# A retention-and-feed-forward kernel: pieces as two halves of 64 tokens, with all their matmuls in four 64x64 tiles

## The chip, the cores and the metric

The kernel runs on one core of a Trainium2 chip. The metric is device time in microseconds: the median of several runs of the whole program, inputs and outputs in HBM. A profiled execution of the kernel before gives the trace; "the profile" is its page, and the views named below (the chain that ended last, groups of instructions, waits, timeline) are answers of that trace.

## The reference

Inputs `q`, `k`, `v` have 8 sequences (batch), 8 heads, 576 tokens and 64 dimensions a head, in fp32. The kernel computes a retention (attention without softmax, decaying with distance) and feeds it to a dense block with a hard-swish:

```python
scores = scale * np.matmul(q, k.transpose(0, 1, 3, 2))          # scale = 1/8
gamma = 1.0 - 2.0 ** (-5.0 - np.arange(H))                      # one decay for each head
rel = pos[:, None] - pos[None, :]
Dmat = np.where(rel >= 0, gamma[:, None, None] ** rel[None, :, :], 0.0)
attn = np.matmul(scores * Dmat, v)                              # B, H, S, D
x = attn.transpose(0, 2, 1, 3).reshape(B * S, H * D)            # 4608 x 512
h = x @ w_in                                                    # 512 x 2048
out = (h * np.clip(h + 3.0, 0.0, 6.0) / 6.0) @ w_out            # 2048 x 512
```

## The kernel before

**Dense part.** The 4608 tokens are nine blocks of 512 (blocks 0 to 7 are the first 512 tokens of each sequence, block 8 holds the last 64 tokens of all eight). For each block `gemm1` runs 16 units `g1` (four 512-column matmuls, L401, into a PSUM bank `ph`; ScalarE's `u` L408 and VectorE's `gt` L409 form the activation), and 16 units `g2` follow (four 512-column matmuls, L459, into `pout`; after four units ScalarE copies `pout` to `osb`, L463, and SP stores it). The operands are fp16.

**Attention part.** The tokens are 36 pieces of 128: four main pieces for each sequence, and four rest pieces (12, 21, 30, 35) that hold the last 64 tokens of two sequences each. Because the decay is a power of the distance, a piece needs its own scores under a causal mask and a running state (keys times scaled values, a 64x64 matrix for each head) of the pieces before it. Four pairs of heads share the 128 partitions. For a piece the kernel does:

- `scores`: 8 matmuls of 128 columns, 64 rows by 128 columns of the array (L302, and L583 for the second piece of a pair), then the mask on VectorE (`at`, L306 or L591);
- `inter`: state times queries, with the state laid out block-diagonally in `tbd` so that both heads of a pair go through one 128x128 matmul (L324);
- `intra`: 8 matmuls of 128 columns, 128 rows by 64 columns of the array (L335), accumulated onto `inter`, then one ScalarE copy to `xt16` (L341);
- `update_mm`: 8 matmuls of 64 columns, 128 rows by 64 columns (L359), and `update_state`: an add and a scaling on VectorE (L375, L376), and two ScalarE copies of the state into `tbd` (L388, L389).

**Order.** It is written out by hand; the engines run their queues in order, and TensorE's order is the order of the code. Pieces 0 to 3 (`EARLY`) run first, while loads arrive: their Q and K are transposed on TensorE (`k_by_pe` L215, `q_by_pe` L224), piece 3 has forms of its own (`scores_last`, `out_last`), and the state is summed in PSUM by an identity matmul (`state_early`, L273 and L277) and multiplied by `gfull` (L282). `warm` matmuls (L174) fill gaps. Then comes `gemm1(0)`. Pieces 4 to 7 are worked between the `g2` units of block 0 by `first_step`, and the first units of block 1 are split into a group of 384 and one of 128 columns (`g1_columns`, L424), the first of which needs only pieces 4 to 6. Pieces 8 to 35 are worked in pairs by `step(ended, begun)` between the `g2` units of the block before theirs, at the positions in `AT`; a pair never spans two blocks, so a block of five pieces has a last step for one. A step does `inter` of the ended pieces, `scores` of the begun ones, `intra` of the ended, then the update of the begun. Their Q and K are transposed by DMA from SP (`ahead`), at the last units of the block before.

**Buffers.** PSUM has eight banks: two for `sc`, one each for `o` and `tu`, and four that turn under the name `ph`. Loads (`load`, L91, POOL's queue) have six buffers for `kn` and `qv`.

Of the kernel before, what the change touches and what calls it, by code (L numbers as in the profile page):

```python
# [17 lines left out]
def kernel(  # L18
# [111 lines left out]
    mask01 = mask_wide[:, 1:P + 1]  # L130
    ident16 = const.tile([P, P], FP16)
# [16 lines left out]
    gfull = const.tile([P, NPAIR, P], FP32)  # L148
    nc.vector.memset(gfull, 0.0)

    def fill_gfull():
        nc.scalar.copy(gfull[0:HALF, :, 0:D],
                       gc[0:HALF, 0, :, None].to_broadcast([HALF, NPAIR, D]))
        nc.scalar.copy(gfull[HALF:P, :, D:2 * D],
                       gc[HALF:P, 0, :, None].to_broadcast([HALF, NPAIR, D]))

# [3 lines left out]
    tbd = []  # L160
    for i in range(5):
        t = const.tile([P, NPAIR, P], FP16, name=f"tbd{i}")
        if i >= EARLY:
            nc.vector.memset(t, 0.0)
        tbd.append(t)
# [3 lines left out]
    def warm(n, cols):  # L169

        w = psum.tile([P, MBLK], FP32, tag="ph", bufs=4, name=f"warm_{warmed[0]}")
        warmed[0] += 1
        for _ in range(n):
            nc.tensor.matmul(w[:, 0:cols], zeros[:, 0:P], zeros[:, 0:cols],  # L174
                             start=True, stop=True)
# [3 lines left out]
    mask_rest = const.tile([P, P], FP16)  # L179

    def make_mask_rest():
        nc.vector.tensor_copy(mask_rest, mask01)
        nc.vector.memset(mask_rest[0:HALF, HALF:P], 0.0)

    mask_b = {"main": mask01[:, None, :].to_broadcast([P, H, P]),
              "rest": mask_rest[:, None, :].to_broadcast([P, H, P])}
# [3 lines left out]
    later = []  # L190
    free_tbd = list(range(5))
    state_of = {}

    def run_later(n):
        for _ in range(n):
            if later:
                later.pop(0)()

    def scale_v(c):
        vs = work.tile([P, 2, H, D], FP16, tag="vs", bufs=6, name=f"vs_{c}")  # L200
        st.setdefault(c, {})["vs"] = vs[:, 1]
        nc.vector.tensor_tensor(out=vs[:, 1], in0=loaded[c]["qv"][:, 1], in1=gqv[:, 1],  # L202
                                op=ALU.mult)

    def qk_of(c):
        if "qk" not in st.setdefault(c, {}):
            st[c]["qk"] = work.tile([P, 2, NPAIR, P], FP16, tag="qk", bufs=6, name=f"qk_{c}")
        return st[c]["qk"]

    def k_by_pe(c, tag="ph"):  # L210
        kn = loaded[c]["kn"]
        pk = psum.tile([P, NPAIR, P], FP16, tag=tag, bufs=4 if tag == "ph" else 1,
                       name=f"trk_{c}")
# [4 lines left out]
    def q_by_pe(c):  # L218
        q16, qk = loaded[c]["q16"], qk_of(c)
        pq = psum.tile([P, NPAIR, P], FP32, tag="ph", bufs=4, name=f"trq_{c}")  # L220
# [11 lines left out]
    def scores_last(c):  # L232

        qk = st[c]["qk"]
        sc = psum.tile([P, 2, NPAIR, P], FP32, tag="sc", name=f"sc_{c}")
        at = work.tile([P, 2, NPAIR, P], FP16, tag="at", bufs=4, name=f"at_{c}")
        st[c]["at"] = at
        for p in range(NPAIR):
            for h2 in range(2):
                r = slice(h2 * HALF, h2 * HALF + HALF)  # L240
                nc.tensor.matmul(sc[:, h2, p, :], qk[r, 1, p, :], qk[r, 0, p, :],
                                 start=True, stop=True)
        for p0 in (0, 2):
            nc.vector.tensor_tensor(  # L244
                out=at[:, :, p0:p0 + 2, :], in0=sc[:, :, p0:p0 + 2, :],
                in1=mask01[:, None, None, :].to_broadcast([P, 2, 2, P]), op=ALU.mult)

    def out_last(c):
        before, qk = st[c]["before"], st[c]["qk"]
        at, vs = st[c]["at"], st[c]["vs"]  # L250
        g0 = column_of(c)
        halves = [psum.tile([P, NPAIR, P], FP32, tag="o", name=f"o_{c}"),
                  psum.tile([P, NPAIR, P], FP32, tag="ph", bufs=4, name=f"o2_{c}")]
        for i, o in enumerate(halves):
            for p in range(2):
                nc.tensor.matmul(o[:, p, :], tbd[before][:, 2 * i + p, :], qk[:, 0, 2 * i + p, :],
                                 start=(p == 0), stop=False, skip_group_check=True)
        for i, o in enumerate(halves):
            for p in range(2):
                for h2 in range(2):  # L260
                    r = slice(h2 * HALF, h2 * HALF + HALF)
                    nc.tensor.matmul(o[r, p, :], vs[:, 4 * i + 2 * p + h2, :],
                                     at[:, h2, 2 * i + p, :],
                                     start=False, stop=(p == 1), skip_group_check=True)
            nc.scalar.copy(xt16[:, 2 * i:2 * i + 2, g0:g0 + P], o[:, 0:2, :])

    def state_early(c):

        kn, vs = loaded[c]["kn"], st[c]["vs"]
        u = psum.tile([P, NPAIR, P], FP32, tag="tu", name=f"u_{c}")  # L270
        old = st[c]["before"] = state_of.get(0)
        for p in range(NPAIR):
            nc.tensor.matmul(u[:, p, :], kn[:, 2 * p:2 * p + 2, :], vs[:, 2 * p:2 * p + 2, :],  # L273
# [432 lines left out]
```

## Time and profile before

| | us |
|---|---|
| median of 3 runs | 307.89 (307.84 to 308.3) |
| profiled execution, its own time | 308.26 |
| its span, first to last instruction | 306.4 |
| TensorE busy | 298.6 |
| VectorE busy | 185.1 |
| ScalarE busy | 174.3 |
| pieces 0 to 3, until the first dense matmul | 0 to 19.14 |
| dense units of block 0 before the first output unit | 19.14 to 33.06 |
| output units of block 0 with pieces 4 to 7, first columns of block 1 | 33.06 to 57.63 |
| the rest of block 1, then blocks 2 to 8 with pieces 8 to 35 | 57.63 to 302.5 |

The profiled execution's own time is 1.86 us above its span. A line of the chain gives the start, the length and the work that the end waited for at that time; in a group's line, "128*64 128x128" means 128 rows and 64 columns of the array and a moving operand of 128 partitions by 128 columns, then the count, the busy time and the mean duration in ns. A matmul's duration counts until its result is through, so that durations of matmuls overlap.

### The profile page before, as it was taken

What the parts mean: (1) busy time and instruction counts of PE and PEld (TensorE: products, weight loads), DVE (VectorE), ACT (ScalarE), POOL (GpSimd) and SP (SyncE); (2) the same over time, 40 slices, a digit from 0 to 9 for tenths busy, and PEclk for the clock granted to TensorE, in tenths of its full rate; (3) what the DMA queues carried; (4) which work ended last, traced back from release to release, by engine and by line L of the source; (5) the groups of instructions that cost most, each with busy time, mean ns of one, the idle gap of its engine ahead of it and who ended that gap; (6) DMA issues with size and microseconds to landing.
All of it is one profiled execution on the core that took longest, in us unless ns stands there. A gap on an engine that the chain in (4) does not pass through costs nothing.

```text
span 306.4 us, 5769 instructions
## 1 busy us (share of the span) xinstructions
PE 298.6 (97%) x2239; PEld 150.2 (49%) x2239; DVE 185.1 (60%) x309; ACT 174.3 (57%) x301; POOL 107.9 (35%) x134
## 2 busy tenths in 40 slices
PE   6999999999999999999999999999999999999994
PEld 2654455544544554445545544455445544444443
DVE  4668427795857872776477728856787358207700
ACT  5568437883567454754574638544865477227611
POOL 8963477178630590065133830257000000000000
PEclk9999999999999999999999999999999999999999
DMA  9999999999999999369999996199920120011022
GB/s 66 147 200 205 190 162 210 171 119 152 181 163 157 86 145 161 94 42 157 179 131 90 145 174 135 8 164 141 139 71 36 68 68 2 34 68 36 1 68 68
DMA packets 153164, 35.51 MB, mean 116 GB/s; under 512 B 143793, under 2 KB 148657, under 8 KB 153137
## 3 DMA queue, kind: packets, MB, share of 16 engines
q0 software_dynamic: 117264, 18.36, 85.3%
q1 hardware_dynamic: 35472, 16.26, 25.8%
q10 hardware_dynamic: 400, 0.52, 0.5%
q8 instruction: 17, 0.28, 0.4%
q14 instruction: 11, 0.08, 0.1%
HBM read 36.70 MB, written 9.44 MB: 151 GB/s over the span
## 4 chain that ended last, share of the span: by engine, by line
PE 95%; DMA 1%; DVE 1%; issue 1%; ACT 1%; POOL 0%; POOLq 0%
PE pout L459 40%; PE ph L401 39%; PE o L335 3%; PE sc L302 3%; PE o L324 2%; DMA qv<-in_q_dram 1%; PE u L359 1%; PE ph L424 1%; PE pout L472 1%; PE trq L224 1%; PE sc L583 1%; PE trk L215 1%; PE u L273 0%; DVE at L244 0%; ACT qk L230 0%
## 5 line engine op out<-in xcount | busy, mean ns | idle before, releaser
L409 DVE SCALAR_TENSOR_TENSOR gt<-u,ph 128x512 f16<-128x512 f32 x144 | 97.9, 687 | 63.2 <-ACT u L408 62.7
L459 PE MATMUL pout<-wout,gt 128*128 128x512 f16 x560 | 126.0, 379 | 0.0
L401 PE MATMUL ph<-xt,win 128*128 128x512 f16 x560 | 122.3, 379 | 0.0
L408 ACT ACTIVATE u<-ph,cb 128x512 f32<-128x512 f32 x144 | 98.2, 687 | 25.2 <-PE ph L401 24.3
L401 PEld LDWEIGHTS <-win 128*128 128x128 f16 x560 | 54.7, 98 | 65.7
L459 PEld LDWEIGHTS <-gt 128*128 128x128 f16 x560 | 52.7, 98 | 60.8
L91 POOL DMA_DIRECT2D kn<-in_k_dram x40 | 34.9, 875 | 94.2 <-PE u L359 67.5
L463 ACT COPY osb<-pout 128x512 f32<-128x512 f32 x35 | 20.5, 586 | 48.9 <-PE pout L459 48.6
L306 DVE TENSOR_TENSOR at<-sc,mask_wide 128x1024 f16<-128x1024 f32 x19 | 23.2, 1222 | 28.5 <-PE sc L302 28.4
L91 POOL DMA_DIRECT2D qv<-in_q_dram x40 | 34.9, 878 | 4.0 <-DMA wout<-in_moe_w_out_dram 3.4
L91 POOL DMA_DIRECT2D qv<-in_v_dram x40 | 35.1, 885 | 2.7 <-DMA wout<-in_moe_w_out_dram 1.7
L388 ACT COPY tbd<-ts 64x256 f16<-64x256 f16 x28 | 11.3, 405 | 32.7 <-DVE ts L372 16.9
L341 ACT CAST xt<-o 128x512 f16<-128x512 f32 x35 | 19.4, 589 | 5.9 <-PE o L335 4.1
L291 DVE TENSOR_TENSOR vs<-qv,gqv 128x1024 f16<-128x1024 f16 x28 | 17.9, 685 | 3.5 <-DMA qv<-in_v_dram 3.5
L591 DVE TENSOR_TENSOR at<-sc,mask_wide 128x512 f16<-128x512 f32 x24 | 15.3, 681 | 0.0
L335 PE MATMUL o<-at,vs 128*64 128x128 f16 x280 | 12.4, 225 | 0.5 <-DVE vs L202 0.5
L389 ACT COPY tbd<-ts 64x256 f16<-64x256 f16 x28 | 11.2, 402 | 0.4
L335 PEld LDWEIGHTS <-vs 128*64 128x64 f16 x280 | 8.7, 111 | 4.0 <-DVE vs L202 2.1
L375 DVE TENSOR_TENSOR ta<-u,ts 128x256 f32<-128x256 f32 x21 | 8.7, 415 | 2.5 <-PE u L359 2.5
L376 DVE TENSOR_TENSOR ts<-ta,gc 128x256 f16<-128x256 f32 x21 | 8.9, 426 | 1.7
L302 PE MATMUL sc<-qk 64*128 64x128 f16 x184 | 9.6, 225 | 0.4 <-ACT qk L230 0.3
L324 PEld LDWEIGHTS <-tbd 128*128 128x128 f16 x112 | 7.0, 98 | 4.0
(69 smaller groups left out, 118.3 us busy)
## 6 DMA issues: line engine op xcount, KB each, us to landing
out_dram<-osb SPq DMA_DIRECT2D x32, 256.0 KB, 4.1
kn<-in_k_dram POOLq DMA_DIRECT2D x32, 128.0 KB, 4.6
qv<-in_q_dram POOLq DMA_DIRECT2D x32, 128.0 KB, 5.2
qv<-in_v_dram POOLq DMA_DIRECT2D x32, 128.0 KB, 5.8
wout<-in_moe_w_out_dram POOLq DMA_DIRECT2D x4, 512.0 KB, 15.6
win<-in_moe_w_in_dram POOLq DMA_DIRECT2D x3, 512.0 KB, 10.0
win<-in_moe_w_in_dram POOLq DMA_DIRECT2D x2, 256.0 KB, 6.3
kn<-in_k_dram POOLq DMA_DIRECT2D x8, 64.0 KB, 4.0
```

The costliest lines, as they stand in the source:

```text
L91: loaded[c]["dma"].append(nc.gpsimd.dma_start(dst[p0:p0 + n], src[b, :, s0:s0 + n, :].rearrange("h s d -> s h d")))
L291: scaled = nc.vector.tensor_tensor(out=vs, in0=loaded[c]["qv"], in1=gqv, op=ALU.mult)
L302: nc.tensor.matmul(sc[:, h2, p, :], qk[r, 1, p, :], qk[r, 0, p, :], start=True, stop=True)
L306: later.append(lambda: nc.vector.tensor_tensor(out=at.rearrange("t a b s -> t (a b) s"), in0=sc.rearrange("t a b s -> t (a b) s"), in1=mas ...
L335: nc.tensor.matmul(o[r, p, :], vs[:, 2 * p + h2, :], at[:, h2, p, :], start=(st[c]["first"] and p == 0), stop=(p == NPAIR - 1 and not more ...
L341: nc.scalar.copy(xt16[:, :, g0:g0 + P], o)
L401: nc.tensor.matmul(ph, win16[:, dmc, P * fc:P * fc + P], xt16[:, dmc, t0:t0 + MBLK], start=(dmc == 0), stop=(dmc == NCC - 1))
L408: nc.scalar.activation(u, ph, ACTF.Relu, bias=cb[:, 0:1], scale=1.0 / 6.0)
L409: nc.vector.scalar_tensor_tensor(out=gts[kb][:, fc, :], in0=u, scalar=1.0, in1=ph, op0=ALU.min, op1=ALU.mult)
L459: nc.tensor.matmul(pout, gt[:, fc, P * mc:P * mc + P], wout16[:, fc, :], start=(fc == 0), stop=(fc == NFC - 1))
L463: nc.scalar.copy(osb, pout)
L591: nc.vector.tensor_tensor(out=at[:, h2], in0=banks[h2], in1=mask[:, None, :].to_broadcast([P, NPAIR, P]), op=ALU.mult)
```

## The change

A piece is worked as two halves of 64 tokens. The state of a piece's first half (`lo`) is the one after the piece before; that of its second half (`hi`, tile `tm`) is formed in between. The mask becomes 64x64 (`mask64`), as only the diagonal blocks of a half are left to it, and the states are used as 64-row operands, so `tbd`, `gfull` and `mask_rest` go. All matmuls of scores, inter, intra and update have 64 rows, 64 columns and 64 moving columns: 16 for each, where there were 8, 4, 8 and 8. The four quarters of the array take scores, intra and update in turn; inter uses the two on the diagonal. Between inter and intra TensorE drains, since they reach the same bank from different rows of the array. Outputs go to two banks, one for each half, and are copied by two ScalarE instructions for a pair (two for each piece where it is alone).

Pieces from 8 on are paired in order, across block edges (from piece 12); the steps have new positions (`steps_at`), 16 instead of 23, and the DMA transposes are spread over earlier units (`ahead_at`). Pieces 4 to 7 are worked by `single`; piece 3's outputs move in among the first columns of block 0. The four turning banks get names, and a bank is pinned while units accumulate into it over several steps. `at` has three buffers instead of four, `qk` and `vs` eight instead of six.

The core of the diff (cut, and without the lines that are only taken out):

```diff
+    mask64 = const.tile([P, HALF], FP16)
+    nc.vector.tensor_copy(mask64[0:HALF], mask_wide[0:HALF, 1:HALF + 1])
+    nc.vector.tensor_copy(mask64[HALF:P], mask_wide[HALF:P, HALF + 1:P + 1])
...
+    def bank(shape, dtype, name, tag=None, pin=False):
+        if tag is None:
+            tag = next(t for t in ring if t not in pinned.values())
+            ring.remove(tag)
+            ring.append(tag)
+            if pin:
+                pinned[name] = tag
+        return psum.tile(shape, dtype, tag=tag, name=name)
...
+    def scores(cs):
+        sc = psum.tile([P, 2, 2, NPAIR, HALF], FP32, tag="sc", name=f"sc_{cs[0]}")
...
+            for p in range(NPAIR):
+                for h2 in range(2):
+                    for half in range(2):
+                        nc.tensor.matmul(sc[rows(half), h2, j, p, :],
+                                         qk[rows(h2), 1, p, rows(half)],
+                                         qk[rows(h2), 0, p, rows(half)], start=True, stop=True)
...
+    def inter(cs, tag=None):
+        o = [bank([P, 2, NPAIR, HALF], FP32, f"o0_{cs[0]}", "o"),
+             bank([P, 2, NPAIR, HALF], FP32, f"o1_{cs[0]}", tag)]
...
+            for half in (1, 0):
+                if states[half] is None:
+                    continue
+                for p in range(NPAIR):
+                    for h2 in range(2):
+                        st[cs[0]]["inter"] = nc.tensor.matmul(
+                            o[half][rows(h2), j, p, :], states[half][rows(h2), p, :],
+                            st[c]["qk"][rows(h2), 0, p, rows(half)],
+                            start=(half, h2) not in written, stop=False, skip_group_check=True)
+                        written.add((half, h2))
+
+    def intra(cs):
+        if "inter" in st[cs[0]]:
+            st[cs[0]].pop("inter")
+            nc.tensor.drain()
+        for j, c in enumerate(cs):
+            o, at, vs, written = st[c]["o"], st[c]["at"], st[c]["vs"], st[c]["written"]
+            for p in range(NPAIR):
+                for half in (1, 0):
+                    for h2 in range(2):
+                        mm = nc.tensor.matmul(
+                            o[half][rows(h2), j, p, :], vs[rows(half), 2 * p + h2, :],
+                            at[rows(half), h2, p, :], start=(half, h2) not in written,
+                            stop=(j == len(cs) - 1 and p == NPAIR - 1), skip_group_check=True)
...
+    def state_half(c, direct=False):
...
+        st[c]["lo"] = before = state_of.get(b)
+        st[c]["hi"] = tm = work.tile([P, NPAIR, D], FP16, tag="tm", bufs=4, name=f"tm_{c}")
+        if direct:
+            nc.vector.tensor_tensor(out=tm, in0=u[0], in1=before, op=ALU.add)
+        st[c]["sum"] = ta = work.tile([P, NPAIR, D], FP32, tag="th", bufs=2, name=f"th_{c}")
+        def whole():
+            if before is None:
+                nc.scalar.copy(ta, u[0])
+            else:
+                nc.vector.tensor_tensor(out=ta, in0=u[0], in1=before, op=ALU.add)
+        if direct:
+            return whole
+        whole()
+        nc.scalar.copy(tm, ta)
+
+    def state_whole(c):
...
+        nc.vector.tensor_tensor(out=ta, in0=st[c]["u"][1], in1=st[c]["sum"], op=ALU.add)
+        nc.vector.tensor_tensor(out=ts, in0=ta, in1=scale, op=ALU.mult)
+        state_of[b] = ts
...
     for c in range(EARLY):
         k_by_pe(c)
         warm(1, MBLK)
         q_by_pe(c)
         if c == 0:
             warm(1, MBLK)
         else:
+            inter([c - 1])
+        mask = scores([c])
+        if c > 0:
+            intra([c - 1])
+            outputs([c - 1])
+        update_mm([c])
+        mask()
+        rest_of_half = state_half(c, direct=(c == EARLY - 1))
         if c < EARLY - 1:
+            state_whole(c)
             scale_v(c + 1)
...
+    def single(c):
+        old, new = c - 1 >= EARLY, c + 1 < 8
         if new:
             q_by_pe(c + 1)
+        if old:
+            inter([c - 1])
+        mask = scores([c])
+        if old:
+            intra([c - 1])
+            outputs([c - 1])
+        update_mm([c])
+        load_until(min(c + NBUF, 11))
         if new:
+            scale_v(c + 1)
+        state_half(c)
+        mask()
+        state_whole(c)
...
     def step(ended, begun):
+        if ended:
+            inter(ended)
         if begun:
+            mask = scores(begun)
+        if ended:
+            intra(ended)
+            outputs(ended)
+        if begun:
+            update_mm(begun)
+            load_until(begun[-1] + NBUF)
+            for c in begun[:-1]:
+                state_half(c)
+                state_whole(c)
+            state_half(begun[-1])
+            mask()
+            state_whole(begun[-1])
...
+    banks = [g1_bank(0, fc, pin=True) for fc in range(2)]
+    g1_columns(0, 0, banks[0], done)
+    inter([EARLY - 1])
+    intra([EARLY - 1])
+    outputs([EARLY - 1])
+    rest_of_half()
+    state_whole(EARLY - 1)
+    g1_columns(0, 1, banks[1], done)
+    for fc in range(2):
+        g1_columns(0, fc, banks[fc], last)
     gemm1(0, {9: [(fill_gq,)]})
...
+        {3: [(q_by_pe, 4), (k_by_pe, 4, "tu"), (scale_v, 4)], 9: [(k_by_pe, 5, "tu")],
+         10: [(single, 4)], 12: [(k_by_pe, 6), (single, 5)], 13: [(k_by_pe, 7)],
+         14: [(single, 6), (transpose_k, 8)], 15: [(single, 7), (transpose_k, 9)]})
+    banks = [g1_bank(1, fc, pin=True) for fc in range(2)]
     for fc in range(2):
         g1_columns(1, fc, banks[fc], done)
+    inter([7], "tu")
+    intra([7])
+    outputs([7])
...
+    pairs = [[c, c + 1] for c in range(8, NP, 2)] + [[]]
+    steps_at = {1: {-1: (-1, 0), 6: (0, 1), 12: (1, -1)},
+                2: {-1: (-1, 2), 3: (2, 3), 7: (3, 4), 11: (4, 5)}, 3: {3: (5, 6), 10: (6, 7)},
+                4: {3: (7, 8), 10: (8, 9)}, 5: {3: (9, 10), 10: (10, 11)},
+                6: {2: (11, 12), 6: (12, 13), 10: (13, -1)}, 7: {}}
+    ahead_at = {1: {4: 12, 8: 13, 13: 14, 14: 15}, 2: {0: 16, 1: 17, 4: 18, 5: 19, 13: 20, 14: 21},
+                3: {0: 22, 1: 23, 13: 24, 14: 25}, 4: {0: 26, 1: 27, 13: 28, 14: 29},
+                5: {0: 30, 1: 31, 12: 32, 13: 33, 14: 34, 15: 35}, 6: {}, 7: {}}
```

## The prediction

> **What bounds the kernel now.** I read the page first, for the busy shares and the chain that ended last, then that chain in order of time, then the groups of instructions kept apart by shape, and last the waits.
>
> ```profile
> span 306.4 us, 5769 instructions
> PE 298.6 (97%) x2239; PEld 150.2 (49%) x2239; DVE 185.1 (60%) x309; ACT 174.3 (57%) x301; POOL 107.9 (35%) x134
> PE 95%; DMA 1%; DVE 1%; issue 1%; ACT 1%; POOL 0%; POOLq 0%
> ```
>
> TensorE is busy for 97% of the span and is 95% of the chain. From 19 us on, a change is worth what it adds to or takes from TensorE's stream, so long as no new wait appears. The chain in order of time (start, length, what) shows what the attention costs there:
>
> ```profile
> 75.92 0.22 PE o L324 x4
> 76.15 0.33 PE sc L302 x8
> 76.48 0.22 PE sc L583 x8
> 76.70 0.57 PE o L335 x16
> 77.27 0.25 PE u L359 x16
> 77.52 4.42 PE pout L459 x20
> ```
>
> This is one step for a pair of pieces between dense units. Two things are read from it. Eight score matmuls take 0.33 us where the tile shape has just changed (L324 uses 128x128, L302 64x128) and 0.22 us where it has not (L583): a change of shape costs 0.1 us, and a step has three (into L302, into L335, back to L459). And the 16 update matmuls, 64 columns each in two tiles side by side, take 0.25 us: 15.6 ns each.
>
> The shapes, with count, busy time and mean:
>
> ```profile
> L335 PE MATMUL o<-at,vs 128*64 128x128 f16 x280 | 12.4, 225 | 0.5 <-DVE vs L202 0.5
> L302 PE MATMUL sc<-qk 64*128 64x128 f16 x184 | 9.6, 225 | 0.4 <-ACT qk L230 0.3
> L359 PE MATMUL u<-vs,kn 128*64 128x64 f16 x224 | 6.8, 197 | 0.0
> L375 DVE TENSOR_TENSOR ta<-u,ts 128x256 f32<-128x256 f32 x21 | 8.7, 415 | 2.5 <-PE u L359 2.5
> L265 ACT CAST xt<-o 128x256 f16<-128x256 f32 x2 | 0.7, 373 | 1.1 <-PE o L262 1.1
> ```
>
> Tiles already overlap in pairs: side by side (L335, L359) and one above the other (L302). A single 64-column matmul lasts 197 ns from issue to end, though 15.6 ns pass between issues. The start is another regime:
>
> ```profile
> 14.70 0.40 PE sc L302 x8
> ...
> 17.10 0.37 PE sc L241 x8
> 17.47 0.02 issue
> 17.50 1.30 DVE at L244 x2
> 18.80 0.04 issue
> 18.84 0.30 PE o L262 x4
> 19.14 13.92 PE ph L401 x64
> ```
>
> Pieces 2 and 3 have their scores 2.4 us apart, TensorE-paced; then VectorE's mask is waited for, and dense work starts at 19.14. Weights set a floor below this: the first part of W_in is issued at 11.9 us and such parts take 6.3 us to land, so 1.5 us at most could be gained here. I count a difference under 0.2% (0.6 us) as none, about what a measurement of this kernel can tell.
>
> **Late pieces 8 to 35 (from 67.99 us).** Before: adding all attention entries of the chain gives 3.53 us for each of three four-piece blocks, 4.44 for each of three five-piece blocks and 0.91 for the last piece: 24.8 us in 23 steps. After: scores 28x16 = 448 matmuls, intra 448, update 24x16 = 384, inter 28x16-6x8 = 400 (the first pieces of six sequences have no state for their first half): 1,680 instead of 752, all with 64 columns. The inter matmuls use only the two diagonal tiles, as L359 uses two: 15.6 ns each, 6.2 us. The other 1,280 can use four tiles. No row shows four; half of the pair rate is 7.8 ns, no overlap beyond pairs is 15.6. Since pairs overlap in both directions I take it near the lower end, 9 ns: 11.5 us. Shape changes: 16 steps with two each, 3.2 us.
>
> The drain between scores and intra is new: 14 times here. TensorE must finish its last matmul (the 197 ns row, of which about 9 would have passed anyway), be released (0.04 us, as at 18.80), and then refill a queue that is empty, which no row shows. Lower end 0.1 us (a change of shape, which waits for the array as well), upper end 0.4; I take 0.3, since the first two terms alone are 0.23. Queued behind it are intra, the update and the dense units; the output copies and the state wait for those. 14x0.3 = 4.2 us. Sum 6.2+11.5+3.2+4.2 = 25.1, so +0.3 us: the saved matmul time goes into drains.
>
> The Trainium skill speaks against the 9 ns: TensorE: Matmul & The Clock Gate, section Back-to-back issue gap, puts a floor of about 25 ns under any matmul of 1 to 64 columns. At 25 ns, 1,680 matmuls would be 42 us and the late part +24 us; the 15.6 ns of L359 disagrees with it as soon as two tiles alternate, and the measurement decides.
>
> Off the path: VectorE per pair had masks 1.22+1.36 and four state operations (1.7), now one mask 1.22 and six (2.5), no more than before; ScalarE trades two copies of 0.59 and four of 0.40 for two of 0.59 and two of 0.37. The deepest reuse, a ring bank holding the second update sum, is read within 3.3 us and wanted again after one 3.45 us row of dense units; cover gone would cost its rest, some tenths per step. Transposes move to earlier slots on SP and POOL's loads follow; the tightest is piece 19, loaded after the update near 100 us: values land near 106.5, scaling 0.7 and the transpose's 4.0 us (the page's DMA issues) end near 111.7, and scores want it near 114. I cost these at nothing; 2 us more of transfer would show as a wait.
>
> **Middle, pieces 4 to 7 (33.06 to 57.63, 24.57 us).** Dense work is 64 matmuls of 0.216 and four column groups of 0.87: 17.3 us. The new attention part, summed the same way (Q transposes 0.22, K transposes 0.22, scores, intra and update 0.14 each, inter 0.25, first piece's 0.12, four drains, 15 shape changes): 7.05 us. The stall of L335 on L202 (0.5) goes, since values are now scaled a step ahead. New: after the step of piece 7 the dense columns need piece 6's outputs, whose two ScalarE copies (2x0.37) begin 0.2 us after its intra, while only the update and a shape change (0.24) lie between; before, a whole unit (0.86) covered it. That is 0.75 us, and 0.15 more where the state copy of piece 6 comes late. 25.25, so +0.7 us.
>
> **Start, pieces 0 to 3.** Between the scores of pieces 2 and 3 the path moves to VectorE and ScalarE: scores 0.14 and run-through 0.2, mask 0.68 (512 elements, as L244's halves), state sum 0.42, then on ScalarE the state copy 0.37, K copy 0.59 and Q copies 0.75 in this order, releases 0.15: 3.3 us where it was 2.4. Scores of piece 2 stay near 14.6, those of piece 3 move from 17.10 to 17.9. Piece 2's two output copies end near 19.4, and dense columns start. Between the first two groups TensorE now does piece 3's inter 0.25, drain 0.3, intra 0.14, three shape changes 0.3, and waits 0.25 for its output copies: the two groups end at 22.3, where they ended at 19.14+8x0.216 = 20.87. +1.4 us (0.7 with drains of 0.1). All later work is queued behind it.
>
> **Sum.** +0.3+0.7+1.4 = +2.4 us on the profiled execution's 308.26 us (span 306.4 and 1.9 around it): 310.7. That execution lies 0.37 above the median of the runs, so the median to expect is 310.3.
>
> **Rivals.**
> *Cheap drains (faster).* If a drain costs 0.1 us, as a change of shape does, and four tiles reach 7.8 ns: late 6.2+10.0+3.2+1.4 = 20.8, -4.0; middle -0.35; start +0.7: -3.65, 304.2 us. For it: a shape change waits for the array too and costs only 0.1. Against: a drain also empties the queue. With tiles at 9 ns it decides the sign: below about 0.18 us a drain the kernel is faster.
> *Tiles only two at a time.* All 1,680 at 15.6 ns: late 33.6, +8.8; middle +2.0; start +3.2, half of it with the slow clock of the first 13 us: +14, 322 us. For it: the update rows leave 31 ns between matmuls of one tile, which may be the weight loads and not the array.
> *Feeding.* In the step shown 52 matmuls pass in 1.60 us, 31 ns each; the new step wants 128 in about 1.8 us. The burst of 15.6 ns is 16 long and may come out of a filled queue. If instructions arrive at only 31 ns per matmul, the late part is 1,680x0.031+7.4 = 59.5 us, +35, with +5 each in the middle and at the start: about 350 us. The change would then not do what it says. The Trainium skill names such a limit (Runtime: NRT & Kernel Launch, section Instruction fetch mechanics: an issue floor of about 20 cycles an instruction); with a weight load for each matmul and the sequencer's 1.2 GHz (TensorE: Matmul & The Clock Gate, section Wait — 56ns, not 53.3ns?), I estimate 33 ns per matmul from it, and no run here shows it.
>
> **How the numbers follow.** Forecast (308.5 to 313): 0.45. Cheap drains: 0.27. Two at a time: 0.18. Feeding: 0.10. The predicted time is the forecast's, 310.3. The range reaches from the cheap-drain end to the pair-rate end, 304 to 322, and leaves out feeding and edges, under 0.2; the forecast alone spans 308.5 to 313. Faster: 0.27 and 0.03 of the forecast's lower edge, 0.30. Same: 0.08, from the forecast. Slower: 0.62.
>
> **What would show it.** In the changed profile: late steps of about 1.8 us, two shape changes each, 32 score matmuls in about 0.3 us, and a gap of 0.3 us before each intra; scores of piece 3 near 17.9 and block 0's third dense group near 22.3; ScalarE outputs ending the wait before block 1's first columns. Wrong if the gap before intra is near 0.1, if 32 intra matmuls take 0.5 us or more, if the matmuls after a drain come at the pace of arriving instructions, or if a wait on VectorE or a transpose opens in the late part.

## The result, and the profile after

The changed kernel takes 322.43 us (median of 4 runs, 321.49 to 323.16) against 307.87 us for the kernel before on the same chip (4 runs): a ratio of 1.0469, interval 1.044 to 1.0499, slower. The forecast of 310.3 us had the sign right and the size wrong; the time lies just above the range's end of 322. Where some runs of a kernel lie more than 1.5% above its fastest, the times and ratios below leave them out: two of four runs in warm3, one of four in combined, three of six in hybrid2_dd and in hybrid3 (the traces of these last two are of such a run).

The page after (span, busy times, the clock that the throttle granted in 40 slices, in tenths of full speed, the chain by engine):

```profile
span 321.3 us, 8259 instructions
PE 300.8 (94%) x3476; PEld 150.5 (47%) x3476; DVE 178.6 (56%) x316; ACT 165.2 (51%) x297; POOL 107.8 (34%) x134
PEclk9559999889999999799999999999999999999999
PE 89%; DMA 5%; issue 3%; ACT 1%; POOL 0%; DVE 0%; POOLq 0%; DVEq 0%
```

The clock row of the page before:

```profile
PEclk9999999999999999999999999999999999999999
```

TensorE's busy time grew by 2.2 us, the span by 14.9: TensorE now waits. In the chain there are 5% DMA and 3% "issue" (no releaser in the trace), and the clock row, all nines before, shows half clock in three places. (The row is nine too where the trace has no record of the clock. In the trace before the first record is at 13.3 us, and the K transposes ahead of it take 0.43 us for four, behind it 0.22: that kernel also began at half clock, but left it earlier.) A step for a full pair of pieces, in a quiet part of the trace, looks as it was forecast (chain in order of time):

```profile
161.30 0.56 PE o L281 x28
...
161.93 0.25 PE sc L248 x26
162.18 0.12 issue
162.30 0.45 PE o L297 x32
162.75 0.29 PE u L329 x31
```

L281 is inter, L248 scores, L297 intra, L329 update. 26 score matmuls pass in 0.25 us, the update's 31 in 0.29; the drain is the 0.12 of "issue" with what the array still does at the ends of both neighbours (0.29 to 0.33 us from the start of the last score to that of the first intra matmul, in most late steps). From dense unit to dense unit it is 1.83 us. The loss is elsewhere, and the waits name the places (engine, line, releaser: us in all, times, longest):

```profile
PE sc L248 <- DMA qk<-vs: 5.1, 2, 2.6
PE o L281 <- issue: 2.3, 1, 2.3
PE o L297 <- issue: 1.9, 4, 1.3
```

The chain around the 2.3 us, in the step that ends piece 7:

```profile
58.80 0.34 PE o L281 x14
59.14 2.33 issue
61.47 0.22 PE o L281 x2
...
62.12 3.95 PE ph L397 x24
```

TensorE stops after 14 of 16 matmuls that read the same tiles, and the instructions behind the stop wait for no semaphore: no data is late. Behind it, 24 column matmuls take 3.95 us, because the clock is at half. The windows show it by stage (PEclk is the column after POOL, then DMA share and GB/s):

```profile
7.90:24.90 17.00, 15.54 (x306) 10.19 (x306) 9.52 (x21) 8.66 (x21) 12.89 (x17) 0.50 1.70 177
...
62.50:65.90 3.40, 3.40 (x23) 2.45 (x21) 0.31 (x1) 1.35 (x4) 0.00 (x0) 0.50 0.53 47
```

The third such stretch is 130.8 to 134.2 us, behind a wait of 2.7 us for a transpose.

**Where the 14.9 us went.** I lay one ruler on both traces: from the end of the last dense matmul's columns to the start of the next dense matmul, over each stretch of attention; what the dense stretches are longer is the clock. The start is read at the first output matmul, 32.90 us before and 36.48 after.

| stage | forecast | measured | of it |
|---|---|---|---|
| start, to the first output unit | +1.4 | +3.6 | half clock from 7.9 to 24.9 us: about 2.2 over the forecast |
| middle, pieces 4 to 7 | +0.7 | +4.9 | attention itself +1.0, wait in L281 2.3, dense units at half clock 1.5 |
| late, pieces 8 to 35 | +0.3 | +6.45 | attention itself -2.05, waits 7.1 (two for transposes, one in L297), half clock 1.4 |

The late part's own -2.05 is 25.03 us in 16 steps without waits (measured later, in hybrid2_light) against 27.08 in the 23 steps of before. In all, waits make 9.4 us of the 14.9 and the half clock about 5; what the pieces cost by themselves makes some 0.4. So three things had to be explained: the half clock of the start, the waits without a releaser, and the late transposes.

### The profile page after: what moved, and what is told of

It reads as the page before. It is cut to its first block, busy times and chain, and to the rows that moved or that the text cites. A ratio compares the mean times of both kernels' runs of the same rounds, so it can differ in the third digit from the quotient of the medians.

```text
span 321.3 us, 8259 instructions
## 1 busy us (share of the span) xinstructions
PE 300.8 (94%) x3476; PEld 150.5 (47%) x3476; DVE 178.6 (56%) x316; ACT 165.2 (51%) x297; POOL 107.8 (34%) x134
## 4 chain that ended last, share of the span: by engine, by line
PE 89%; DMA 5%; issue 3%; ACT 1%; POOL 0%; DVE 0%; POOLq 0%; DVEq 0%
PE ph L374 37%; PE pout L424 36%; DMA qk<-vs 4%; PE ph L397 3%; PE o L297 3%; PE o L281 3%; PE sc L248 2%; PE u L329 1%; DMA qv<-in_q_dram 1%; PE trq L219 1%; PE pout L438 1%; PE trk L210 1%; ACT xt L314 1%; ACT qk L225 1%; PE warm L182 0%
## 5 line engine op out<-in xcount | busy, mean ns | idle before, releaser
L351 DVE TENSOR_TENSOR th<-u,ts 128x256 f32<-128x256 f32 x24 | 10.2, 424 | 28.3 <-PE u L329 24.5
L307 ACT CAST xt<-o 128x512 f16<-128x512 f32 x20 | 10.7, 589 | 25.5 <-PE o L297 21.8
L314 ACT CAST xt<-o 128x256 f16<-128x256 f32 x32 | 10.0, 381 | 22.0 <-PE o L297 20.9
L365 DVE TENSOR_TENSOR ta<-u,th 128x256 f32<-128x256 f32 x32 | 13.5, 420 | 13.8 <-ACT th L349 12.5
L254 DVE TENSOR_TENSOR at<-sc,mask 128x1024 f16<-128x1024 f32 x14 | 17.0, 1216 | 3.2 <-PE sc L248 3.2
L355 ACT CAST tm<-th 128x256 f16<-128x256 f32 x31 | 12.7, 410 | 8.6 <-DVE th L351 8.3
L248 PE MATMUL sc<-qk 64*64 64x64 f16 x576 | 10.6, 200 | 5.9 <-DMA qk<-vs 5.1
L297 PE MATMUL o<-at,vs 64*64 64x64 f16 x576 | 9.4, 201 | 4.2 <-issue 1.9
L248 PEld LDWEIGHTS <-qk 64*64 64x64 f16 x576 | 8.5, 111 | 7.4 <-issue 5.1
L281 PE MATMUL o<-qk,ts 64*64 64x64 f16 x256 | 8.7, 197 | 2.3 <-issue 2.3
## 6 DMA issues: line engine op xcount, KB each, us to landing
wout<-in_moe_w_out_dram POOLq DMA_DIRECT2D x4, 512.0 KB, 15.6
```

The costliest lines, as they stand in the source:

```text
L248: nc.tensor.matmul(sc[rows(half), h2, j, p, :], qk[rows(h2), 1, p, rows(half)], qk[rows(h2), 0, p, rows(half)], start=True, stop=True)
L254: nc.vector.tensor_tensor(out=at.rearrange("t a j p s -> t (a j p) s"), in0=sc.rearrange("t a j p s -> t (a j p) s"), in1=mask64[:, None, ...
L281: st[cs[0]]["inter"] = nc.tensor.matmul(o[half][rows(h2), j, p, :], states[half][rows(h2), p, :], st[c]["qk"][rows(h2), 0, p, rows(half)], ...
L297: mm = nc.tensor.matmul(o[half][rows(h2), j, p, :], vs[rows(half), 2 * p + h2, :], at[rows(half), h2, p, :], start=(half, h2) not in writt ...
```

## The experiments

### One suspect at a time, in the changed kernel

**early_transposes.** The scaling of piece 16's queries and values, which its Q transpose needs, stood in VectorE's order behind the masks and states of the step at 109 us, though its loads had landed by 99 us. In the changed kernel VectorE scales pieces 16 and 17 at 112.64 us (first line), and the transpose of 16's queries follows on SP:

```profile
112.64 1.28 DVE L233 TENSOR_TENSOR vs<-qv,gqv 128x1024 f16<-128x1024 f16 x2
```

```profile
113.35 1.20 SPq L234 DMA_TRANSPOSE qk<-vs  x1
```

```diff
-    ahead_at = {..., 2: {0: 16, 1: 17, 4: 18, 5: 19, 13: 20, 14: 21},
+    ahead_at = {..., 2: {3: 19, 13: 20, 14: 21},
-        gemm1(kb + 1, {})
+        gemm1(kb + 1, {0: [(load_until, 18)], 1: [(ahead, 16)], 4: [(ahead, 17)],
+                       15: [(ahead, 18)]} if kb == 1 else {})
```

> Pieces 16, 17 and 18 are scaled and transposed during the third block's first dense layer, 19 after the next step; TensorE's stream is unchanged. Theory (the late part loses its time to a few stalls): the waits of 2.76 and 2.71 us ahead of two score groups at 119.3 and 127.3 us go, and with them the half-clock stretch behind the second (about 1.5 us): about -7.0 us, 315.4. Rival (the transposes are slow because loads share the DMA engines, so they are late wherever they are issued): the waits move to another pair of pieces and at most 2 us is gained, about 320.5. Rival (the attention matmuls and drains themselves are dearer, two tiles at a time): under 1 us.

Measured: 321.45 us, ratio to before 1.0429 (1.0364 to 1.0493): a gain of 1, which the intervals don't tell from none, and a miss for the theory's size; the time is what the first rival gave.

```profile
PE sc L248 <- DMA qk<-vs: 1.9, 1, 1.9
...
PE ph L374 <- DVE gt L382: 1.1, 1, 1.1
```

One of the two transposes' waits went; the other stayed (piece 19, whose loads only began at 112 us, once piece 13 gave its buffer free). A new one came: the scaling of 17, placed too early, held VectorE until its values had landed, and the dense units behind it waited.

**warm3.** `warm(1, MBLK)` becomes `warm(3, MBLK)` in the loop over the first four pieces, and the second call for piece 0 `warm(2, MBLK)`.

> Three instead of one 512-column matmul on zeros per early piece, between its K and Q transposes (one more after the first piece's Q transposes). Theory (the start is lost to TensorE's half clock, which comes of too little work in it): the granted clock stays full from 7.9 us or comes back well before 24.9; the second dense layer of block 0 then begins about 2 us earlier less what the added matmuls cost on the path (0 to 1.3 us): 320 to 321. Rival (the clock doesn't follow the work): the half clock stays to 24.9, and 7 added matmuls of 0.43 us each lie mostly on the path: +2.5 us, 325.

Measured: 318.12 us, 1.0323 (1.0288 to 1.0359): the theory, with 2 us more gained than it said. The first output unit starts at 34.57 instead of 36.48 us:

```profile
5.20:18.70 13.50, 9.92 (x279) 6.00 (x277) 8.41 (x18) 7.85 (x19) 13.32 (x17) 1.00 1.99 157
18.80:22.10 3.30, 3.19 (x42) 1.70 (x41) 0.80 (x2) 0.65 (x2) 1.23 (x2) 0.50 1.25 209
```

The clock is full from 5.1 us, where its record begins, to 18.8 us, and at half in one stretch of 3.4 us instead of five. With that stretch and the added matmuls left in it, the start costs 1.7 us over before, close to the forecast's +1.4.

**shift128.** 64 tiny matmuls, in a bank of the ring, ahead of the first Q transposes.

```diff
+    def shift(n):
+        w = bank([P, MBLK], FP32, "shift")
+        for i in range(n):
+            r = rows(i % 2)
+            nc.tensor.matmul(w[r, 0:8], zeros[r, 0:HALF], zeros[r, 0:8], start=True, stop=True)
...
         warm(1, MBLK)
+        if c == 0:
+            shift(64)
         q_by_pe(c)
```

> 64 tiny matmuls (8 columns, with 64 weight loads, 128 instructions) are put into TensorE's idle time before the first Q transposes; nothing else is changed, so every later instruction stands 128 places further on in its stream. Theory (the gaps of 2.53 us at 58.95 and 1.50 at 91.08 are waits for a block of 256 instructions that is fetched too late): the first gap appears 128 instructions earlier in the order (in the scores or intra matmuls of piece 7 or the step before, about 3 us before), or shrinks; the second goes, since the 256 instructions ahead of the new boundary take over 10 us: -1.5 us at least, 319 to 321. Rival (TensorE waits there for data or for a semaphore): both gaps stay at the same matmuls, and the time stays 322.4.

Measured: 323.49 us, 1.0492 (1.046 to 1.0524); no gain in time, but the wait moved. Chain in order of time (in this file L256 is scores):

```profile
57.18 0.06 PE sc L256 x3
57.24 2.79 issue
60.02 0.28 PE sc L256 x10
```

It now stops between scores of piece 7, in another group of matmuls with other operands, and the wait near 91 us is gone. Counting TensorE's instructions in the trace (matmuls, weight loads, drains and semaphore instructions), it is the same count:

```
kernel             waits without releaser: instructions before it (us)
changed            1473 (2.53)   2240 (1.50)
early_transposes   1473 (3.09)   2240 (1.49)
warm3              1473 (2.25)   2240 (1.02)
shift128           1473 (2.98)
hybrid2 (below)    2240 (1.70)   2496 (0.95)   2752 (2.71)
late_fixed (below)  449 (0.72)   1473 (3.32)   2240 (1.29)   2753 (1.45)   3009 (0.78)
```

All are 192 or 193 modulo 256. TensorE's instructions come in blocks of 256 (16 KB; the page's instruction queue moves 27 packets and 0.44 MB, before 17 and 0.28 MB), and these waits are for a block (a boundary, below, is the place where one block ends and the next begins). The gain of 1.5 us that I expected is there in the late part, whose attention stretches are 1.7 us shorter by the ruler, but it was lost again: the first output matmul starts 1.15 us later (37.63 us), the first wait grew by 0.45, since here too 256 instructions ahead of it are used up in 5.1 us, and one more half-clock stretch follows a wait for a transpose.

**two_tiles.** In scores, intra and update the loop over halves becomes the outer one of a piece, so that 8 matmuls in a row use two tiles.

> The loops of scores, intra and update are reordered so that 8 consecutive matmuls of a piece use two tiles (one half of the tokens) and then 8 the other two; counts, waits and results are the same. Theory (four tiles overlap, 7.8 to 14 ns a matmul, against 15.6 for two): 64-column matmuls go to about 15.6 ns, 1,280 late ones and some 350 early ones by 5 to 8 ns each: +8 to +11 us, about 331, less what slower use of instructions takes off the stalls (up to 4). Rival (they overlap two at a time already): no change, 322.4.

Measured: 324.48 us, 1.051 (1.0473 to 1.0547). Undisturbed steps grew from 1.83 to 1.95 us and from 1.69 to 1.81, some 0.12 for 80 to 96 matmuls, not the 0.6 expected:

```profile
164.64 0.28 PE sc L248 x28
```

28 scores still pass in 0.28 us. So the order of the tiles within 16 matmuls matters little, and this run does not measure the rate of two tiles; L281, which only ever uses two, does: 28 in 0.56 us beside 26 scores in 0.25 (16.1 and 8.5 ns from one start to the next).

### The late part alone, behind the old start

**hybrid_plain, hybrid.** Pieces 0 to 7 take the functions of the kernel before; the end states of sequences 0 and 1 are handed over as 64-row tiles for piece 12. `hybrid` adds a seventh buffer (`bufs=NBUF + 1` for `kn` and `qv`) and puts `ahead` of 16, 17, 18, 19 after units 1, 7, 11, 15 of the third block's first dense layer.

> Pieces 0 to 7 as in the kernel before (128-token pieces, block-diagonal state), pieces 8 to 35 exactly as in the changed kernel. Theory (late part -1.8 us by itself, plus stalls): no loss at the start and in the middle; the two transposes' waits ahead of scores (2.76 and 2.71) and a half-clock stretch (1.5) stay, the instruction-block wait of 1.5 near 91 us may move or go, since fewer instructions stand before it: 307.9 + 5 to 6.5 = 313 to 314.4. Rival (the 64x64 tiles cost in every step): the same time, but spread over all 14 steps, and the next kernel of this call keeps it.

> As hybrid_plain, and pieces 16 to 19 are transposed in the third block's first dense layer, with a seventh buffer for natural tiles so that piece 19 is loaded before it. Theory: all named stalls gone, the late part's own gain of 1.8 us is left: 306.1, up to 307.6 if a wait for an instruction block of 1.5 us remains: at or a little below the kernel before. Forecast of the prediction for the late part (+0.3): 308.2. Rival (tiles cost in every step): 313 or more.

Measured: hybrid_plain 313.62 us, 1.0191 (1.0159 to 1.0224); hybrid 311.86, 1.0108 (1.0062 to 1.0154). The first is as expected; the start's and the middle's losses are gone with the old pieces. The second misses its 306.1 to 307.6: one kind of wait was traded for another (first line hybrid_plain, second hybrid):

```profile
PE sc L264 <- DMA qk<-vs: 4.8, 1, 4.8
```

```profile
PE ph L559 <- DVE gt L567: 2.4, 1, 2.4
```

VectorE stood before the values of 17 in the middle of a dense layer that needs it in every unit.

**combined**, the changed kernel with warm3's matmuls and hybrid's transposes:

> The changed kernel with three warm matmuls per early piece and the transposes of 16 to 19 in the third block's first dense layer, seven buffers. Theory: of the 14.5 us, 2 come back at the start and about 7 in the late part; the wait for an instruction block near 57 us (2.5) with its half-clock stretch (1.6) and the structural 1.4 stay: about 313.5. Rival (stalls move elsewhere): 317 or more.

Measured: 317.13 us, 1.0331 (1.0266 to 1.0395): the rival, at the lower end of its time. The wait at instruction 1473 (2.25) stayed, the one at 2240 (1.24) too, and VectorE held up TensorE by 2.2 us as in hybrid.

**before_nowarm.** The kernel before with `warm(0, MBLK)` in the loop: no such matmuls, the banks turn as before.

> The kernel before without its five 512-column matmuls on zeros in the loop over the first four pieces; nothing else is changed. Theory (the granted clock follows the work in TensorE, whatever the tiles): the first stage stays or falls to half clock well past 13.3 us, as in the changed kernel: +1 to +3 us, 309 to 311. Rival (the 64x64 tiles themselves bring the half clock): full clock from about 13.3 us as before, five matmuls less: 307 to 308.

Measured: 308.1 us, 1.0007 (0.9997 to 1.0016): the rival holds.

```profile
12.50:25.00 12.50, 11.33 (x115) 6.40 (x113) 8.42 (x14) 7.93 (x15) 8.11 (x11) 1.00 1.46 185
```

TensorE is 91% busy here with a full clock, and 91% busy in the changed kernel's 7.9 to 24.9 us with half of it. So the share of busy time in the profile is not what the clock follows. The pieces in 64x64 tiles bring the half clock, and 512-column matmuls among them (warm3) lift it.

What the clock does follow can be read from all 18 traces together. Between two possible changes lie 3.41 us; in each such stretch, weight the columns that every matmul moves with the share of the array that its tile takes (a quarter for 64x64) and sum them, spread over the time in which they pass. A stretch of dense matmuls alone has 8,192. The 50 stretches behind which the clock was at half have 2,896 at most; of the 1,495 behind which it was full, all but one (2,517) have 2,947 or more. The share of busy time doesn't part them: half clock followed 98%, full clock 53%. This was read from the traces afterwards; no run was made to test it.

### What the late steps ask of the instruction stream

**hybrid2, hybrid2_dd.** Scalings where the values have landed; then every drain doubled.

```diff
-                       1: [(ahead, 16)], 7: [(ahead, 17)], 11: [(ahead, 18)], 15: [(ahead, 19)]
+                       4: [(ahead, 16)], 13: [(ahead, 17)]      # and 18, 19 after units 0 and 4 of the second layer
```

> As hybrid, but VectorE's scalings stand where the values have landed: piece 16 after the fifth and 17 after the fourteenth unit of the third block's first dense layer, 18 and 19 in the second layer after the first and the fifth unit. In hybrid, scalings placed too early held up VectorE, and TensorE waited 2.8, 1.0 and 0.5 us for it, with a half-clock stretch of 3.4 us behind the first. Theory (the late part is cheaper by itself, what it lost were waits): these go: 305.5 to 306.3, faster than before by 0.5 to 0.8%. Rival (the DMA engines can't bring four more pieces by 115 us wherever the transposes stand): a wait of 2 to 5 us moves to the scores of piece 17 or 19, 308 to 311.

> As hybrid2, with each of the 14 drains doubled. If a drain's 0.3 us is the time for the array to finish (the second finds it empty): under 0.1 us each, +0.5 to +1.4 us on hybrid2. If it is a price of the instruction itself: +0.3 each, +4.2 us.

Measured: hybrid2 313.88 us, 1.021 (1.0173 to 1.0248), worse than hybrid: a miss for theory and rival. No wait on a transpose or on VectorE is left, steps now follow each other 5 us apart, and instead:

```profile
108.52 1.51 issue
110.03 0.35 PE o L297 x11
...
116.88 0.76 issue
...
121.73 2.33 issue
```

Three waits for instruction blocks in a row, the third among dense matmuls (after the line at 121.73 stands `pout`; in this file L297 is inter). The doubled drains give 310.11 us, 1.011 (1.0059 to 1.0161), less than hybrid2: waits of this kind, which differ from run to run, cover what the drains cost. In the steps after 150 us, where there are none, a step grew from 1.83 to 1.91 us at full clock: a second drain costs 0.08, which fits that most of a drain's 0.3 is the array finishing.

**hybrid3, hybrid4.** Other positions for these steps: hybrid3 spreads them over two output stages, hybrid4 begins pieces 12, 13 and 18, 19 inside the first dense layers.

```diff
...
-  2: {-1: (-1, 2), 3: (2, 3), 7: (3, 4), 11: (4, 5)}, 3: {3: (5, 6), 10: (6, 7)}
+  2: {-1: (-1, 2), 4: (2, 3), 9: (3, 4), 13: (4, -1)}, 3: {1: (-1, 5), 6: (5, 6), 11: (6, 7)}     # hybrid3
+  2: {1: (2, 3), 7: (3, 4), 13: (4, -1)}, 3: {3: (5, 6), 10: (6, 7)}      # hybrid4
+  # and step([], [12, 13]), step([], [18, 19]) after unit 8 of the first layers of blocks 2 and 3 (kb + 1)
...
```

> As hybrid2, with the steps of the third block's second dense layer further apart: after units -1, 4, 9 and 13 (the last ends pieces 16 and 17 only), and pieces 18 and 19 begun a block later. In hybrid2 three waits for instruction blocks (1.7, 0.95 and 2.7 us) with two half-clock stretches lay there, with steps 5 us apart. Theory (a block of 256 instructions that is used up faster than its successor is fetched, 7 to 10 us there, stalls TensorE): steps are now 6 us apart, so part of the waits stays: 307 to 310. Rival (the waits have another cause than the pace of instructions): still 312 to 314.

> As hybrid2, with pieces 12 and 13 begun inside the third block's first dense layer and 18 and 19 inside the fourth's, so that steps there are 6 to 9 us apart. Theory: the waits for instruction blocks shrink to 0 to 1.5 us; new is VectorE's work of two steps (3.7 us each) inside a stage in which it has 0.2 us to spare per unit of 0.86, which may hold up TensorE by 0 to 2 us: 305.5 to 308. Rival (the waits have another cause): 312 to 314.

Measured: hybrid3 314.63 us, 1.0229 (1.0173 to 1.0286), just above its rival's 312 to 314 and not the theory's 307 to 310: waits of 1.4 and 3.6 us stayed at 2240 and 2496, and the transposes of 22 and 23 came too late (4.8 us). hybrid4, with steps 6 to 9 us apart: 310.07, 1.0084 (1.0052 to 1.0116), 2 us above the theory's upper end; one block wait of 1.55 and 1.4 for VectorE are left. Spacing helps; 6 us is not enough.

**hybrid2_light.** Is it the loads that hold up the fetch? This kernel leaves out seven of eight heads in the loads of pieces 18 to 26, so its output isn't the reference's and its time is only for comparison.

```diff
+        heads = 1 if 18 <= c <= 26 else H
...
+            if heads < H:
+                nc.gpsimd.memset(dst[:, heads:], 0.0)
...
-                    dst[p0:p0 + n], src[b, :, s0:s0 + n, :].rearrange("h s d -> s h d")))
+                    dst[p0:p0 + n, 0:heads], src[b, 0:heads, s0:s0 + n, :].rearrange("h s d -> s h d")))
```

> As hybrid2, but of pieces 18 to 26 only one of eight heads is loaded; the other heads are filled with zeros by GpSimd, so that their part of the result is not computed from the inputs. TensorE's stream, the steps 5 us apart and the transposes are as in hybrid2. Theory (the fetch of a block of instructions waits behind the loads in the DMA engines): from 100 to 125 us the fetches start 1 to 3 us after their boundary instead of 4.5 to 9.6, the waits of 1.7, 0.95 and 2.7 us go with their half-clock stretches: 305 to 307. Rival (the fetch takes that long by itself, or the waits come from the data): 312 to 314, waits at the same instructions.

Measured: 306.03 us, 0.9927 (0.9902 to 0.9952): the theory, number and mechanism. The same stretch of the DMA view, 104 to 124 us, hybrid2 first (queue: packets, MB, time that its packets took as a share of the 16 engines' time, over 100% where packets overlap):

```profile
q0 software_dynamic: 14195, 1.78, 153.2%
```

```profile
q0 software_dynamic: 2425, 0.27, 22.3%
```

Queue 0 has GpSimd's loads. The records of the instruction queue beside the count of TensorE's instructions (us):

```
                 boundary passed   next block fetched   its boundary: wait
changed          1216 at  53.72     58.16 to  59.88     1473 at  58.95: 2.53
changed          1984 at  84.26     89.91 to  91.19     2240 at  91.08: 1.50
hybrid2          1984 at 103.23    107.58 to 108.64     2240 at 108.33: 1.70
hybrid2          2496 at 117.64    121.63 to 122.68     2752 at 121.35: 2.71
hybrid2_light    1984 at 103.94    104.72 to 106.21     2240 at 109.19: none
hybrid2_light    2240 at 109.19    109.31 to 110.46     2496 at 114.19: none
before           1472 at  94.34     94.01 to  94.95     1728 at 107.10: none
```

With the loads a fetch begins 4 to 6 us after the boundary, without them after less than 1; work resumes 1.4 to 1.6 us after the block has arrived. The kernel before takes 10.3 us or more over any 256 instructions, the changed one 5.2 and 6.8 in the two stretches that end in a wait. The same holds in all 18 traces: wherever TensorE reached a boundary before its block had arrived or up to 1.3 us after, it went on only 1.3 to 1.7 us after the arrival; where it came 1.4 us or more after the arrival, it did not wait for the block.

**hybrid5, hybrid6.** Steps after units 0, 6 and 14, pieces 18 and 19 begun between the fourth block's layers; hybrid6 also moves the transposes of 22 and 23 into that block's first layer.

> As hybrid4, with the steps after units 0, 6 and 14 of the third block's second dense layer, and pieces 18 and 19 begun between the fourth block's two dense layers, where VectorE has room. In hybrid4 a wait for an instruction block of 1.55 and one for VectorE of 1.8 us were left. Theory: both go or shrink under 0.5 us, and the late part's own gain shows: 306 to 307.3, faster than before by 0.2 to 0.7%. Rival (a wait stays somewhere in the stretch of loads): 308.5 to 311.

> As hybrid5, with the transposes of pieces 22 and 23 moved into the fourth block's first dense layer; in hybrid5 their late scaling left one wait of 1.7 us ahead of scores at 146 us. Theory (late part 1.5 to 2 us cheaper by itself): 306.2 to 307.2, faster than before by 0.2 to 0.6%. Rival (the late part is worth nothing by itself, as the forecast's +0.3 says): 308 or more.

Measured: hybrid5 308.17 us, 1.0007 (0.998 to 1.0035), above the theory's 306 to 307.3, with one wait left:

```profile
PE sc L264 <- DMA qk<-vs: 1.5, 1, 1.5
```

hybrid6 307.59 us, 0.9978 (0.9965 to 0.9991): faster than both kernels, by 0.2% over the one before (at the edge of what the prediction counts as a difference), 0.4 us short of what I expected. Its clock row is all nines.

Its late stretches of attention come to 25.64 us by the ruler (27.08 before); an extra step with its shape changes and one wait of 0.5 us at instruction 2241 separate them from the 25.03 of hybrid2_light.

**late_fixed**, the changed kernel with hybrid6's late schedule:

> The changed kernel, first eight pieces included, with the late schedule of hybrid6 (steps further apart, transposes of 16 to 23 moved, seven buffers). Theory: the late part's 6.5 us go and turn into its gain of about 1.5; the start (3.6) and the middle (4.9, with its wait for an instruction block and the half-clock stretch behind it) stay: 314 to 315.5. Rival (the early losses push the late part into new waits): 317 or more.

Measured: 320.03 us, 1.0378 (1.0355 to 1.0402): the rival. The transposes' waits are gone, but the longer instruction stream ahead puts the boundaries elsewhere, and there are five block waits (7.6 us in the table above, two of them in the late part's new positions). A schedule that is clean behind one start is not behind another.

## Why the prediction was wrong, by its own steps

What failed is the assumption that the new stream meets no wait and keeps its clock: waits cost 9.4 us and the half clock about 5, and the prediction had both at nothing. That the kernel is clearly slower comes from these two; by themselves the pieces cost some 0.35 us (1.4 at the start if the forecast is taken for it, 1.0 in the middle, -2.05 late) where the forecast had 2.4. So the right sign is in the main luck.

- **Four tiles at 9 ns, three shape changes, 0.3 us a drain.** Right: 8.1 to 8.9 ns from start to start, steps of 1.83 us against "about 1.8", 0.29 to 0.33 us from scores to intra. The model's 25.1 us for the late steps stands beside 25.03 measured without waits.
- **"+0.3 us" for the late part.** Its other side was mis-sized: 24.8 us for the 23 old steps, added up from the chain's entries. There the 0.1 us by which a step begins late is booked to the dense group ahead of it, 23 times; in the new steps I counted it as a shape change. By one ruler the old steps are 27.08 us, so the late part was worth -2.05. (The groups of pieces 8 to 35 have 744 old matmuls, not 752; no sum uses the number.)
- **"Transposes ... I cost these at nothing", with piece 19 checked by hand.** This failed. I followed the loads and the transposes' duration, but not VectorE's queue: the scaling of 16 stood behind a whole step there, and SP's four pairs of transposes behind it. The prediction did say that 2 us more would show as a wait; two waits of 2.7 us did.
- **Feeding.** The rival had the right object and the wrong unit. It asked for the pace of single instructions (31 ns a matmul would have been 350 us), and single instructions keep up with 8 ns, far from the 33 of the prediction's estimate. What does not keep up is blocks of 256 while loads fill the DMA engines. The Trainium skill (Runtime: NRT & Kernel Launch, section Instruction fetch mechanics) describes these 256-instruction blocks and calls the cost of crossing one mostly hidden; before agrees, the changed kernel does not, with 1.5 to 2.5 us at two of 27 crossings.
- **Clock.** No step of the prediction asked what the clock would do. It cost 2.2 us over the forecast at the start and about 3 behind the waits. In this trace its changes lie whole multiples of 3.41 us apart (7.88, 24.95, 62.49, 65.91, 130.76, 134.17), and a wait costs a half-clock stretch when it takes too much of the work out of one: the 2.5 us at 58.95 did, the 2.7 at 119.3, which lies across a limit, did not. The Trainium skill (TensorE: Matmul & The Clock Gate, section What's actually happening) gives a free-running window of 3413 ns, which agrees.
- **Start +1.4, middle +0.7.** 1.7 with most of the half clock gone (warm3, whose first two column groups end at 22.6 us, forecast 22.3), and 1.0 for the attention of the middle by the ruler; close, and buried under the rest.
- **Two at a time, 322 us.** Its number came out, its mechanism did not: no run shows 15.6 ns for scores, intra or update. A time that fits a rival is not yet that rival.

What stays open is whether the weighted columns are exactly what the throttle counts, and why a fetch waits for up to 6 us among the loads: that the loads make it late is shown, how they do is not.

## What to carry to other kernels

When a change cuts work into more and smaller instructions, count instructions per microsecond in every stretch where the DMA engines are full, and set 256 of them against the time that a fetch takes there; spread such bursts, or lighten the loads under them. When a transposed or scaled operand moves, follow its whole queue on every engine that touches it, and compare old and new steps with the same ruler. Check the clock that the new form keeps: a stretch that is as busy as before can still lose half of it.

## What the runs showed that I had not expected

- A fetch of a block of instructions (16 KB) began 4 to 6 us after the boundary, ahead of the waits shown, when loads filled the DMA engines, and under 1 us after it with the loads cut; TensorE resumed 1.3 to 1.7 us after it had arrived.
- At 91% busy, TensorE's clock was full with 128-token pieces and half with pieces in 64x64 tiles; columns weighted with the tile's share of the array tell the two apart, with the limit between 2,896 and 2,947 in 3.41 us.
- 8 matmuls in a row on two tiles cost only 0.12 us a step more than four tiles in turn, and a second drain 0.08 us.
